# A second order of all operations of a recurrent-attention and max-out kernel

## Chip, cores and metric

The kernel runs on one core of a Trainium2 chip. The metric is the time of one execution on the device in microseconds (us), the median over runs. Lower is better.

## The reference

A recurrence with a state of 48x48 per batch and head goes through 768 steps (4 batches, 8 heads), and its output goes through a two-branch product with a maximum:

```python
for t in range(S):                                   # S = 768
    cur = einsum('bhd,bhe->bhde', u * k[t], v[t])
    y[t] = einsum('bhd,bhde->bhe', r[t], state + cur)
    state = w[t][..., None] * state + einsum('bhd,bhe->bhde', k[t], v[t])
x = y.transpose(0, 2, 1, 3).reshape(B * S, H * D)    # 3072 x 384
out = maximum(x @ w1, x @ w2) @ w_out                # d_ff = 1024
```

Inputs and outputs are float32.

## The kernel before

The sequence is cut into three chunks of 256 tokens. A unit of work is one chunk of one or two batches: units 0 to 3 are the first chunk of one batch each, unit 4 and 5 the second chunk of two batches each, 6 and 7 the third. The maximum is rewritten: `max(a, b) = relu(a - b) + b`, so that one product with `w1 - w2` (wd_sb) and a relu are followed by a product with w_out and one with `w2 @ w_out` (wc_sb), which the kernel works out itself once (wfold).

Nothing is ordered by a scheduler. A list of words, ORDER, names every operation and every load. A loop goes through it and issues each one to its engine, and each engine works through its own queue strictly in that order, waiting at the first operation whose inputs or buffer aren't there yet. The letter behind the @ chooses the engine where there is a choice (a is ACT, d is DVE, p is POOL):

```python
for o in ORDER:
    o, _, e = o.partition("@")
    name, *a = o.split(".")
    a = [int(x) if x.isdigit() else x for x in a] + ([e] if e else [])
    if name in ops:
        ops[name](*a)
    else:
        unit[name](U[a[0]], *a[1:])
```

The first number behind a unit's operation is the unit; the others are the batch in the unit, a half of the heads (unit 0 is done in halves) or a part. The operations, in the order in which a unit needs them, and the lines under which the profile has them:

- load.n.x: a load of w, k, r or v by SP's queue (L372). row and wl: one row of sums goes to memory and comes back on partitions (L472, L478). dt: a transpose by DMA (L582), in units 5 to 7. os: a store of the output (L743). All of these are in SP's one queue.
- hot.8: eight matmuls of 512 columns on zeros, whose result nobody reads (L234). They read the state buffer S_b that zero.s.0 clears (L263).
- zero.M, zero.k, zero.r, zero.v, zero.s, zero.m: buffers cleared once (L249 to L263). ident, tri, mask, identb, identq, trih: constants.
- wp: product of neighbouring w (L176, L180). ln: its logarithm on ACT (L387). ex: prefix sums by a matmul with a triangle on TensorE (L398; from unit 3 on two half-precision parts hi and lo, L395 and L396). mz: sums plus own logarithm on DVE (L440). e0 and ie: exponentials on ACT (L436, L460). wt, we: the decay over the chunk turned onto partitions by TensorE and its exponential by ACT, for units 0 and 1 (L466, L486); for the others we reads what wl brought (L488).
- rk, ru, dg, dd, di: the terms with u; dg is a row sum on DVE (L502), dd widens it, di sets it on the diagonal of the mask buffer M on DVE (L516). rw and kw: products with w. scale.n.0 and scale.n.1: r and k times their exponentials, into rp and kp. All of these products have the helper lines L176 and L180.
- vb: v to bf16. tr: transposes on TensorE (L565), and te: their copies on ACT. kv: keys times values (L596). st, sm, sb: the state carried on (L612, L615; S_f, S_b).
- sc: scores on TensorE into a Y buffer (L641). mk: the masked copy of them into M on DVE (L650). yi and ya: the output of the recurrence from the state and from M (L675, L688). xe: its copy xT (L168).
- wload, woload: loads of the three weight matrices. w2turn, w2take: w2 transposed. wdiff: w1 - w2 in three parts, wd_sb. wocast: w_out to bf16 in four parts, wo_sb. wfold, wctake: w2 @ w_out in three parts (L318) and their copies. u, uspread, utake: u on all partitions (L270).
- gt: xT times wd_sb (L706), which needs all three parts of wd_sb. rl: the relu (L717 on ACT, L719 on DVE). op: xT times wc_sb and gT times wo_sb (L725, L729). oe: the copy of its result (L168).

Two kinds of PSUM buffers serve TensorE: G has four (hot, ex, tr, w2turn, wfold, gt, op), Y has two (sc, kv, and the outputs of yi and ya). A buffer is taken again when the last operation that reads it is done.

Each ya multiplies 16 or 32 small tiles, each tr 8, each kv 32 or 64, each sc 16 (8 in unit 0), each gt 6 or 3, each op 11. A line of DVE, ACT or POOL at 168, 176 or 180 is that of the helper copy or mul, so the tile's name tells the operations apart.

Of the kernel before, what the change touches and what calls it, by code (L numbers as in the profile page):

```python
# [73 lines left out]
sc.2.0.1.0 mk.2.0.1.0 gt.0.1 mz.3.0 e0.3.0 kw.3.0@p gt.1.0 dg.3 sc.2.0.0.0 kv.2 st.2.0@a rl.0.1@a  # L74
wp.4.0@d ie.3.0 scale.3.0.0.0@d mk.2.0.0.0 wfold.2 sb.2.1@d wfold.0 dd.3@p ln.4.0 load.3.v st.2.1
wfold.1 sb.2.0@d vb.3.0@a wl.2 hi.4@a lo.4@d ya.2.0.0.0 load.4.r rl.1.0@a di.3.0@d vb.3.1@a row.3
ya.2.0.1.0 wctake.1@a we.2 load.4.k wctake.2@a rk.4.0@d wctake.0@a scale.3.1.0.0@p tr.3.0.0 ex.4.0
mz.4.0 tr.3.0.1 ex.4.1 mz.4.1 te.3.0.0@a kv.3 te.3.0.1@a st.3.0@a yi.2.0 xe.2.0@d ie.4.0 op.1.1
oe.1.1@a st.3.1 load.4.v e0.4.0 sb.3.0@a ru.4.0@d gt.2.0 load.5.w.0 rl.2.0@a sc.3.0.0.0 sc.3.0.1.0
vb.4.1@a gt.2.2 op.1.0 rk.4.1@p rw.4.0@d kw.4.0@d scale.4.0.0.0@d scale.4.1.1.0@d scale.4.1.0.0@p  # L80
e0.4.1 rl.2.2@a scale.4.0.1.0@d op.0.1 sb.3.1@a row.4 oe.1.0@a tr.4.1.0 te.4.1.0@a tr.4.1.1 vb.4.0@a
op.0.0 sm.2@p wl.3 mk.3.0.0.0 ya.3.0.0.0 mk.3.0.1.0 ya.3.0.1.0 yi.3.0 oe.0.1@d ru.4.1@p wp.5.0@p
we.3 sm.3@p te.4.1.1@a gt.2.1 xe.3.0@a dg.4 ln.5.0 oe.0.0@d tr.4.0.1 te.4.0.1@a gt.3.0 rl.3.0@a
rl.2.1@a hi.5@a dd.4@d load.5.k kv.4 di.4.0@d sc.4.1.1.0 load.5.r load.5.v rk.5.0@d gt.2.3 rl.2.3@a
gt.3.2 tr.4.0.0 di.4.1@d te.4.0.0@a mk.4.1.1.0 gt.3.3 st.4.0 st.4.1 os.1.0 rl.3.3@a gt.3.1 rl.3.1@a
ru.5.0@p sc.4.1.0.0 rk.5.1@p sc.4.0.0.0 load.6.r sb.4.0@a vb.5.1@a op.2.1 load.6.w.0 lo.5@d wl.4
ex.5.0 mk.4.0.0.0 os.0.0 sb.4.1@a mk.4.1.0.0 oe.2.1@a mz.5.0 e0.5.0 rw.5.0@p ex.5.1 sc.4.0.1.0
load.6.k ru.5.1@p mz.5.1 ya.4.0.0.0 scale.5.0.0.0@d op.2.0 rl.3.2@a op.3.0 mk.4.0.1.0 e0.5.1 os.1.1
scale.5.0.1.0@d dt.5.0.0 ya.4.0.1.0 dt.5.0.1 kw.5.0@d row.5 oe.3.0@d os.3.0 wp.6.0@p ie.5.0
# [19 lines left out]
rl.6.4@a op.6.0 sc.7.1.0.0 sb.7.0@a sc.7.1.1.0 op.6.2 di.7.1@d mk.7.1.1.0 op.6.3 yi.7.1 mk.7.1.0.0  # L109
yi.7.0 ya.7.0.0.0 oe.6.2@a ya.7.1.0.0 ya.7.1.1.0 ya.7.0.1.0 xe.7.0@d op.6.1 oe.6.3@a os.6.3 oe.6.0@d  # L110
os.5.3 os.6.2 oe.6.1@d xe.7.1@a gt.7.1 rl.7.1@d gt.7.0 gt.7.6 os.6.0 rl.7.0@a gt.7.2 gt.7.3 rl.7.2@a
rl.7.6@a rl.7.3@a os.6.1 gt.7.4 rl.7.4@a gt.7.7 rl.7.7@d gt.7.5 rl.7.5@d op.7.0 op.7.1 oe.7.0@d
# [685 lines left out]
```

## Time and profile before

| | |
|---|---|
| time, three runs | 146.47, 146.53, 146.93 us; median 146.53 |
| profiled execution | span 147.2 us from the first to the last instruction (no other time is given for it) |
| granted TensorE clock, mean | 0.987 |
| busy | PE 136.8 us, DVE 116.9, ACT 90.6, POOL 90.0 |
| queue of the loads and stores | 31.49 MB, its packets took 81.2% of the span of 16 DMA engines |

The page gives busy time and instructions by engine, then the span in 40 equal slices with the busy tenths of each, then the chain of work that ended last and the costliest groups by line. Rows of a timeline give start, duration, engine, line, operation, the tile written and read, and in square brackets the idle time ahead with what ended it. Rows of windows give the stretch and its length, then busy time of PE, PEld, DVE, ACT and POOL with the number of instructions, the granted clock, the share of the DMA engines and GB/s. Matmuls of one row overlap a little, so the start of the next row says when a row was done.

### The profile page before, as it was taken

What the parts mean: (1) busy time and instruction counts of PE and PEld (TensorE: products, weight loads), DVE (VectorE), ACT (ScalarE), POOL (GpSimd) and SP (SyncE); (2) the same over time, 40 slices, a digit from 0 to 9 for tenths busy, and PEclk for the clock granted to TensorE, in tenths of its full rate; (3) what the DMA queues carried; (4) which work ended last, traced back from release to release, by engine and by line L of the source; (5) the groups of instructions that cost most, each with busy time, mean ns of one, the idle gap of its engine ahead of it and who ended that gap; (6) DMA issues with size and microseconds to landing.
All of it is one profiled execution on the core that took longest, in us unless ns stands there. A gap on an engine that the chain in (4) does not pass through costs nothing.

```text
span 147.2 us, 5536 instructions
## 1 busy us (share of the span) xinstructions
PE 136.8 (93%) x2403; PEld 84.2 (57%) x2404; DVE 116.9 (79%) x162; ACT 90.6 (62%) x164; POOL 90.0 (61%) x106
## 2 busy tenths in 40 slices
PE   5999999779999999999999994999999999999990
...
DVE  2489999999999999999999967399967589361511
...
PEclk9999999999999999999999999599999999999999
...
GB/s 104 323 325 357 335 401 394 366 286 304 214 241 277 212 226 282 312 255 174 205 192 177 292 251 207 141 138 291 250 136 78 131 271 20 0 210 62 4 56 157
DMA packets 71186, 31.84 MB, mean 216 GB/s; under 512 B 66293, under 2 KB 70390, under 8 KB 71162
## 3 DMA queue, kind: packets, MB, share of 16 engines
q1 hardware_dynamic: 71162, 31.49, 81.2%
...
## 4 chain that ended last, share of the span: by engine, by line
PE 41%; DVE 35%; issue 6%; POOL 6%; DMA 4%; ACT 3%; SPq 2%; DVEq 0%; POOLq 0%; ACTq 0%
PE G L729 12%; DVE M L650 9%; PE G L706 8%; PE G L234 7%; PE G L725 5%; DVE rp L176 4%; DMA lv<-in_v_dram 4%; DVE rku L176 3%; DVE dg L502 3%; POOL kp L180 3%; DVE M L516 3%; PE Y L688 2%; SPq L582 2%; POOL rku L180 2%; PE Y L675 2%
## 5 line engine op out<-in xcount | busy, mean ns | idle before, releaser
L729 PE MATMUL G<-wo_sb,gT 128*128 128x384 bf16 x192 | 35.8, 331 | 0.0
L706 PE MATMUL G<-xT,wd_sb 128*128 128x256 bf16 (+1 forms) x192 | 34.4, 326 | 0.7 <-ACT xT L168 0.6
L650 DVE CAST_PREDICATED M<-mask,Y 128x1024 bf16<-128x1024 int32 (+1 forms) x26 | 28.6, 1131 | 2.8 <-PE Y L641 1.9
L717 ACT ACTIVATE gT<-G 128x512 bf16<-128x512 f32 x43 | 24.5, 601 | 9.8 <-PE G L706 9.6
L729 PEld LDWEIGHTS <-gT 128*128 128x128 bf16 x192 | 19.0, 99 | 12.6 <-issue 0.3
L706 PEld LDWEIGHTS <-wd_sb 128*128 128x128 bf16 x192 | 17.9, 98 | 12.6 <-DVE wd_sb L176 0.6
L180 POOL TENSOR_TENSOR kp<-lk,iE 128x384 bf16<-128x384 f32 x16 | 17.1, 1096 | 9.3 <-DVE lk L176 4.2
L725 PE MATMUL G<-wc_sb,xT 128*128 128x384 bf16 x72 | 15.7, 327 | 0.0
L180 POOL TENSOR_TENSOR rku<-rku,u_b 128x384 f32<-128x384 f32 x14 | 14.5, 1053 | 2.0 <-DVE rku L176 2.0
L234 PE MATMUL G<-S_b 128*128 128x512 bf16 x47 | 13.6, 442 | 1.8 <-DVE S_b L263 1.8
L168 ACT COPY RK<-G 128x1024 bf16<-128x1024 bf16 x12 | 12.1, 1019 | 4.7 <-PE G L565 4.7
L168 ACT COPY osb<-G 128x384 f32<-128x384 f32 x7 | 3.4, 479 | 15.9 <-PE G L729 12.6
L180 POOL TENSOR_TENSOR rku<-lr,lk 128x384 f32<-128x384 f32 x8 | 10.9, 1393 | 2.5 <-DMA lk<-in_k_dram 1.7
L641 PE MATMUL Y<-RK 48*64 48x128 bf16 x384 | 9.0, 220 | 2.6 <-DVE M L650 2.4
L502 DVE TENSOR_REDUCE dg<-rku 128x16 f32<-128x768 f32 x12 | 11.0, 945 | 0.1
L641 PEld LDWEIGHTS <-RK 48*64 48x64 bf16 x384 | 6.2, 106 | 7.8 <-issue 6.7
L168 ACT CAST xT<-Y 128x768 bf16<-128x768 f32 x7 | 7.0, 1025 | 5.3 <-PE Y L675 4.0
L168 ACT CAST S_b<-S_f 64x768 bf16<-64x768 f32 (+1 forms) x14 | 8.7, 624 | 2.3 <-DVE S_f L612 2.0
L176 DVE TENSOR_TENSOR rp<-lr,G 128x768 bf16<-128x768 f32 (+2 forms) x11 | 8.8, 799 | 1.4 <-ACT G L436 1.4
L234 PEld LDWEIGHTS <-S_b 128*128 128x128 bf16 x48 | 5.1, 112 | 8.3 <-issue 3.3
L516 DVE TENSOR_TENSOR M<-identq,gd 128x512 int32<-128x512 int32 x12 | 9.2, 778 | 0.4 <-POOL gd L168 0.3
L168 DVE CAST xT<-Y 128x768 bf16<-128x768 f32 x5 | 5.1, 1017 | 5.5 <-PE Y L688 3.2
(111 smaller groups left out, 240.2 us busy)
## 6 DMA issues: line engine op xcount, KB each, us to landing
...
```

The source lines that it names most:

```text
L168: (nc.scalar.copy if e == "a" else nc.vector.tensor_copy if e == "d" else nc.gpsimd.tensor_copy)(o, i)
L176: op(o, a, b)
L180: op(o[:, g], a[:, g], b[:, g])
L234: nc.tensor.matmul(t, zz[:, 0:P], zz[:, 0:512], start=True, stop=True)
L502: nc.vector.reduce_sum(s.dg[:, b].rearrange("p i h -> p h i"), s.rku[:, b], axis=AX.X)
L516: (nc.vector if en == "d" else nc.gpsimd).tensor_tensor(out=o, in0=m, in1=g.unsqueeze(3).to_broadcast([P, 2, H, Q // 2]), op=ALU.bitwise_and)
L641: nc.tensor.matmul(t[q * Q:(q + 1) * Q, e, p * P:(p + 1) * P].rearrange("s (i g) -> s i g", i=2), s.kT[d, b, j, y * n + p, q, :], s.rT[d, ...
L650: nc.vector.copy_predicated(t[:, :, 2 * n * y:2 * n * (y + 1)].rearrange("s i (p e) g -> s p e i g", e=2), mask[:, j].bitcast(I32).unsquee ...
L706: nc.tensor.matmul(t[:, m * n * P:(m + 1) * n * P].rearrange("c (b t) -> c b t", t=P), wd_sb[:, ko, fo * P:(fo + 1) * P], s.xT[:, 0:n, ko, :],
L717: nc.scalar.activation(o, i, AF.Relu)
L725: nc.tensor.matmul(t[:, 0:HD], s.xT[:, a, ko, :], wc_sb[:, ko, :], start=(ko == 0), stop=False)
L729: nc.tensor.matmul(t[:, 0:HD], s.gT[:, c:c + P], wo_sb[:, f, :], start=False, stop=(f == FO - 1))
```

## The change

The same 652 words stand in another order, and 89 of them carry another letter for their engine. Nothing else changes: the functions, the buffers, the arithmetic and the loads are the same. This is the diff, cut to the beginning (up to the first of the big products), unit 5 and 6, and the last tenth or fifth.

```diff
--- before.py
+++ after.py
@@ -51,66 +51,66 @@
 ORDER = """
-ident zero.s.1@p identq@a load.0.k load.0.r zero.m@p identb@p u zero.s.0@d zero.r@d rk.0.0@d
-load.0.w.1 load.0.w.0 wp.0.0@d hot.8.2 hot.8.3 load.2.w.0 zero.v.1@d wp.0.1@d mask ln.0.0 tri
-zero.k.1@p load.1.w.0 ln.0.1 ex.0.0 load.1.r kw.0.0@d mz.0.0 wp.2.0@d rw.0.0@d load.1.k zero.o@p
-load.0.v ie.0.0 uspread utake@a wp.1.0@d ex.0.1 ln.1.0 wload.1.0 mz.0.1 scale.0.1.0.0@p hot.8.0
-zero.M.1@p ie.0.1 load.3.w.0 ru.0.0@d dg.0 rw.0.1@p kw.0.1@p scale.0.1.0.1@p wt.0.0 ex.1.0 we.0.0
-e0.0.0 e0.0.1 wt.0.1 rk.1.0@d hot.8.5 vb.0.1@p load.2.r zero.v.2@d load.2.k load.1.v mz.1.0 ie.1.0
-rw.1.0@d wt.1.0 wload.1.2 ln.2.0 ex.2.0 vb.0.0@a we.0.1 scale.0.0.0.0@d zero.k.0@d kv.0
-scale.0.0.0.1@d tr.0.0.1 dd.0@p mz.2.0 woload.0 we.1.0 ru.1.0@p kw.1.0@p row.2 w2turn.0.0 e0.1.0
-scale.1.0.0.0@d st.0.0@a tr.0.0.0 te.0.0.1@a sc.0.0.1.1 sc.0.0.0.1 w2turn.0.1 dg.1 te.0.0.0@a
-w2take.0.0@a wload.0.2 load.2.v scale.1.1.0.0@d dd.1@p sb.0.0@a wp.3.0@p tr.1.0.1 e0.2.0 st.0.1
-te.1.0.1@a rk.2.0@d zero.M.2@p di.0.0@d ie.2.0 zero.M.0@p rw.2.0@d hot.8.1 wload.1.1 ru.2.0@d
-kw.2.0@p scale.2.1.0.0@p sc.0.0.1.0 sc.0.0.0.0 mk.0.0.1.0 vb.1.0@a hot.8.4 mk.0.0.0.0 mk.0.0.1.1
-mk.0.0.0.1 vb.1.1@a kv.1 scale.2.0.0.0@d tr.1.0.0 ln.3.0 te.1.0.0@a w2turn.2.1 wdiff.2@p sb.0.1@a
-st.1.0@a sb.1.0@a di.1.0@d st.1.1 tr.2.0.0 w2take.0.1@a tr.2.0.1 te.2.0.1@a zero.v.0@d sc.1.0.1.0
-w2turn.1.0 wload.0.0 wdiff.0@p w2take.1.0@a sc.1.0.0.0 mk.1.0.1.0 mk.1.0.0.0 sb.1.1@a w2take.2.1@d
-w2turn.2.0 w2turn.1.1 w2take.2.0@a hi.3@a ya.0.0.1.0 vb.2.1@a ya.1.0.0.0 sm.0@p sm.1@p wload.0.1
-wdiff.1@d ya.1.0.1.0 ya.0.0.0.1 load.3.r trih@a yi.1.0 yi.0.0 ya.0.0.0.0 woload.1 ya.0.0.1.1
-xe.1.0@a xe.0.0@d load.3.k te.2.0.0@a gt.1.3 rl.1.3@a dg.2 rk.3.0@d lo.3@d dd.2@a gt.0.2 rl.0.2@a
-wocast.1@p gt.1.1 w2take.1.1@d woload.3 gt.0.0 rw.3.0@p woload.2 rl.0.0@a gt.1.2 load.4.w.0 rl.1.2@a
-vb.2.0@p ru.3.0@p gt.0.3 rl.0.3@a ex.3.0 wocast.3@d wocast.2@a wocast.0@a rl.1.1@a di.2.0@d
...
-vb.5.0@a gt.4.7 rl.4.7@a we.4 sm.4@p gt.4.4 dt.5.1.0 gt.4.6 sc.5.0.1.0 mk.5.0.1.0 kv.5 oe.3.1@a
-rl.4.6@a rl.4.0@a rl.4.4@a st.5.0 gt.4.1 rl.4.1@a sc.5.0.0.0 mk.5.0.0.0 gt.4.3 rl.4.3@a dt.5.1.1
-rk.6.1@p st.5.1 ex.6.0 ru.6.1@p sb.5.1@a sb.5.0@a load.6.v os.0.1 vb.6.1@a mz.6.0 ex.6.1 op.4.3
-load.7.w.0 load.7.k mz.6.1 e0.6.1 ie.6.0 kw.6.0@d e0.6.0 scale.6.1.1.0@p di.5.1@d sc.5.1.0.0
-ya.5.0.1.0 rw.6.0@d ya.5.0.0.0 yi.5.0 xe.5.0@a vb.6.0@a scale.6.0.0.0@d op.4.2 wl.5 os.3.1
-scale.6.1.0.0@p sc.5.1.1.0 oe.4.2@a op.4.0 oe.4.3@a oe.4.0@a mk.5.1.0.0 wp.7.0@p ya.5.1.0.0
-mk.5.1.1.0 dt.6.0.0 ya.5.1.1.0 yi.5.1 kv.6 scale.6.0.1.0@d dt.6.0.1 xe.5.1@d st.6.0 dt.6.1.1 ln.7.0
...
-ya.6.0.1.0 os.5.2 os.4.0 ya.6.1.0.0 ya.6.0.0.0 oe.5.3@a os.4.3 kw.7.0@p scale.7.1.1.0@p
-scale.7.0.0.0@d ya.6.1.1.0 yi.6.0 xe.6.0@a scale.7.1.0.0@d dt.7.0.0 dt.7.1.0 yi.6.1 op.5.0 vb.7.0@p
-xe.6.1@a gt.6.5 oe.5.0@d os.5.0 e0.7.1 gt.6.3 rl.6.3@a rl.6.5@a scale.7.0.1.0@d dt.7.1.1 gt.6.2
-dt.7.0.1 os.4.2 kv.7 gt.6.6 gt.6.0 rl.6.6@a os.5.1 st.7.0 gt.6.1 rl.6.2@a ru.7.1@p dg.7 sb.7.1@a
-gt.6.7 rl.6.7@a rl.6.0@d sc.7.0.0.0 rl.6.1@a dd.7@p di.7.0@d sc.7.0.1.0 mk.7.0.1.0 mk.7.0.0.0 gt.6.4
...
+zero.M.0@d ident mask zero.o@p zero.k.0@d zero.s.0@d hot.8.2 load.0.r zero.m@p zero.r@p load.0.w.1
+load.0.w.0 identq@a wp.0.0@d wp.0.1@d ln.0.0 ln.0.1 zero.k.1@d load.0.k identb@p rw.0.0@d hot.8.0
+rk.0.0@d tri ex.0.0 mz.0.0 ex.0.1 mz.0.1 e0.0.1 load.2.w.0 wp.2.0@d zero.v.2@d kw.0.0@d ie.0.0
+scale.0.1.0.0@d hot.8.3 ie.0.1 u load.1.w.0 rw.0.1@d wt.0.1 kw.0.1@p wp.1.0@p scale.0.1.0.1@p
+load.0.v load.1.r uspread e0.0.0 scale.0.0.0.0@d utake@d zero.v.0@d scale.0.0.0.1@d hot.8.1 ln.2.0
+ex.2.0 ru.0.0@d wt.0.0 dg.0 dd.0@d load.1.k load.2.k we.0.0 ln.1.0 vb.0.1@d ex.1.0 rw.1.0@p kw.1.0@p
+mz.1.0 load.2.r tr.0.0.0 wload.1.2 load.1.v we.0.1 rk.1.0@d vb.0.0@a kv.0 tr.0.0.1 wload.1.1
+wload.1.0 te.0.0.0@a wt.1.0 we.1.0 di.0.0@d ru.1.0@d te.0.0.1@a ie.1.0 e0.1.0 sc.0.0.0.0 vb.1.0@a
+zero.s.1@p st.0.0@d sb.0.0@a sb.0.1@a mz.2.0 dg.1 e0.2.0 sc.0.0.1.0 woload.3 row.2 dd.1@a
+scale.1.0.0.0@d st.0.1 scale.1.1.0.0@p ie.2.0 hot.8.5 vb.1.1@a hot.8.4 w2turn.2.0 mk.0.0.1.0
+w2take.2.0@a kv.1 st.1.0@a sb.1.0@a tr.1.0.1 te.1.0.1@a w2turn.1.0 tr.1.0.0 load.3.w.0 wload.0.2
+mk.0.0.0.0 te.1.0.0@a w2turn.1.1 w2take.1.1@a zero.M.1@d st.1.1 wocast.3@a w2turn.2.1 w2take.1.0@a
+w2take.2.1@a rk.2.0@p kw.2.0@p sc.1.0.1.0 ru.2.0@p sc.1.0.0.0 di.1.0@d w2turn.0.1 sb.1.1@a
+w2take.0.1@a rw.2.0@d scale.2.1.0.0@d scale.2.0.0.0@d tr.2.0.1 w2turn.0.0 mk.1.0.1.0 mk.1.0.0.0
+woload.1 wocast.1@a ya.0.0.0.0 sc.0.0.0.1 sc.0.0.1.1 mk.0.0.1.1 tr.2.0.0 w2take.0.0@d te.2.0.0@a
+yi.0.0 mk.0.0.0.1 te.2.0.1@a dg.2 dd.2@a wp.3.0@p woload.2 wocast.2@p wload.0.0 woload.0 load.3.r
+wocast.0@a wdiff.2@p wload.0.1 wfold.2 wctake.2@a trih@a wfold.0 yi.1.0 ya.1.0.0.0 di.2.0@d
+ya.1.0.1.0 wdiff.0@d xe.1.0@a ln.3.0 wctake.0@a load.3.k wfold.1 rk.3.0@p kw.3.0@p sm.0@p ya.0.0.1.0
+wdiff.1@d ya.0.0.0.1 ya.0.0.1.1 hi.3@a gt.1.2 xe.0.0@d rl.1.2@a gt.1.1 load.3.v vb.3.0@a gt.0.1
+rl.1.1@a wctake.1@d load.2.v vb.2.1@a gt.1.0 rl.1.0@a vb.2.0@a load.4.w.0 lo.3@d load.4.r gt.1.3
+rl.1.3@a ex.3.0 ru.3.0@d gt.0.2 dg.3 dd.3@a sm.1@p sc.2.0.1.0 mz.3.0 e0.3.0 kv.2 st.2.0@a zero.M.2@d
+mk.2.0.1.0 rl.0.1@a load.4.k sb.2.1@a ie.3.0 op.1.1 sb.2.0@a wp.4.0@d di.3.0@d vb.3.1@a op.1.0
+rw.3.0@p ln.4.0 hi.4@a row.3 oe.1.1@d scale.3.0.0.0@d scale.3.1.0.0@p st.2.1 gt.0.0 rl.0.2@a
...
+sc.5.0.0.0 mk.5.0.1.0 mk.5.0.0.0 gt.4.7 e0.6.1 rl.4.7@a op.4.3 ex.6.0 di.5.1@d sc.5.1.0.0 os.2.1
+oe.4.3@a sc.5.1.1.0 op.4.2 mz.6.0 ie.6.0 os.0.0 e0.6.0 mk.5.1.0.0 ya.5.0.1.0 rw.6.0@p kw.6.0@p
+sb.5.1@a oe.4.2@a sb.5.0@a load.6.v wl.5 os.4.2 vb.6.1@a op.4.0 oe.4.0@a mk.5.1.1.0 load.7.k
+ya.5.1.1.0 ya.5.1.0.0 ya.5.0.0.0 scale.6.0.1.0@d scale.6.1.0.0@d scale.6.1.1.0@d dt.6.0.1 dt.6.1.1
+yi.5.0 xe.5.0@a wp.7.0@p yi.5.1 xe.5.1@d vb.6.0@a we.5 op.4.1 oe.4.1@a ln.7.0 gt.5.7 load.7.r
+scale.6.0.0.0@d dt.6.0.0 ru.6.1@d kv.6 st.6.0 gt.5.0 ru.6.0@p rl.5.7@a dt.6.1.0 rl.5.0@a dg.6 hi.7@a
+lo.7@d dd.6@d di.6.1@d gt.5.5 gt.5.4 rl.5.4@a os.4.1 rl.5.5@a rk.7.1@p di.6.0@d sb.6.0@d load.7.v
...
+ya.6.1.1.0 ya.6.1.0.0 ya.6.0.1.0 kw.7.0@d ru.7.0@p ya.6.0.0.0 scale.7.0.0.0@d dt.7.0.0 yi.6.0
+vb.7.1@a xe.6.0@a scale.7.1.0.0@p yi.6.1 op.5.0 xe.6.1@d gt.6.1 vb.7.0@a oe.5.0@a gt.6.3 gt.6.6
+ru.7.1@d scale.7.0.1.0@d dt.7.1.0 rl.6.6@a rl.6.3@a gt.6.4 rl.6.4@a scale.7.1.1.0@p kv.7 os.0.1
+gt.6.2 dt.7.0.1 dg.7 gt.6.0 rl.6.0@a sm.5@p st.7.0 sb.7.1@d gt.6.5 rl.6.5@a os.3.0 rl.6.2@a rl.6.1@a
+dd.7@p di.7.0@d sc.7.0.1.0 sc.7.0.0.0 mk.7.0.0.0 dt.7.1.1 gt.6.7 os.4.3 rl.6.7@a mk.7.0.1.0 sb.7.0@d
+op.6.3 oe.6.3@d sc.7.1.0.0 os.5.0 di.7.1@d mk.7.1.0.0 sc.7.1.1.0 op.6.2 op.6.0 yi.7.0 mk.7.1.1.0
+oe.6.0@a oe.6.2@d yi.7.1 ya.7.0.0.0 os.6.0 os.6.3 ya.7.0.1.0 os.4.0 ya.7.1.1.0 ya.7.1.0.0 xe.7.1@d
+op.6.1 xe.7.0@a gt.7.1 rl.7.1@a gt.7.3 rl.7.3@d gt.7.0 rl.7.0@a gt.7.4 gt.7.2 gt.7.5 rl.7.4@a
+oe.6.1@d os.6.1 gt.7.7 rl.7.2@d os.3.1 gt.7.6 os.6.2 os.5.1 rl.7.5@a rl.7.7@d rl.7.6@d op.7.0
+oe.7.0@d op.7.3 oe.7.3@d os.7.3 op.7.2 oe.7.2@a os.7.0 os.7.2 op.7.1 oe.7.1@a os.7.1
 """.split()
```

48 lines of the change are left out of this document (20 added, 28 removed).

## Prediction

> **What bounds the kernel now.** I read the page first, for busy shares and slices.
>
> ```profile
> span 147.2 us, 5536 instructions
> PE 136.8 (93%) x2403; PEld 84.2 (57%) x2404; DVE 116.9 (79%) x162; ACT 90.6 (62%) x164; POOL 90.0 (61%) x106
> PE   5999999779999999999999994999999999999990
> DVE  2489999999999999999999967399967589361511
> PEclk9999999999999999999999999599999999999999
> ```
>
> A slice is 3.68 us. The PE row is open at its two ends, a little around the ninth slice, and in the 25th, behind which the granted clock drops. Elsewhere TensorE has no room. VectorE is as full up to the 22nd slice and empties towards the end. A window of ten microseconds says the same in numbers (its length, then busy us of PE, PEld, DVE, ACT and POOL, the granted clock and the DMA share):
>
> ```profile
> 40.00:50.00 10.00, 10.00 (x208) 6.55 (x201) 9.96 (x16) 9.41 (x20) 6.84 (x6) 1.00 0.99 259
> ```
>
> Then TensorE's timeline, for when the full stretch begins, ends and is broken:
>
> ```profile
> 1.79 6.10 PE L234 MATMUL G<-S_b 128*128 128x512 bf16 x16 [1.79 <-DVE S_b L263]
> 14.66 0.95 PE L466 MATMUL G<-MZ 128*128 128x1 f32 x8
> 15.47 0.89 PE L398 MATMUL G<-lg,tri 128*128 128x384 f32 x2
> 33.11 4.28 PE L706 MATMUL G<-xT,wd_sb 128*128 128x256 bf16 x36 [0.60 <-ACT xT L168]
> 40.02 4.06 PE L318 MATMUL G<-wo_sb,wb 128*128 128x384 bf16 x24
> 87.29 1.46 PE L729 MATMUL G<-wo_sb,gT 128*128 128x384 bf16 x8
> 90.70 0.42 PE L641 MATMUL Y<-RK 48*64 48x128 bf16 x16 [1.94 <-DVE M L650]
> 142.37 1.46 PE L729 MATMUL G<-wo_sb,gT 128*128 128x384 bf16 x8
> ```
>
> So the kernel has three parts. Up to 33.11, when the first gt (the first of the two big products) starts, VectorE's queue sets the pace. From there to 143.83 TensorE runs through its queue with one real hole, at 88.75. The last 3.3 us are a copy and a store. TensorE's work is the same set of operations in both orders, so the new time is settled by when the first gt starts, how much of the queue is then done, and which holes lie behind it.
>
> **The change, part by part.** 28 operations go from POOL to DVE, 18 the other way, 17 from ACT to DVE, 20 back, 5 from POOL to ACT, 1 from ACT to POOL: 89. Priced start to start from the rows below, this gives DVE some 3 us more in all, POOL 12 less, ACT 2.5 more. DVE is not full behind 86 us and POOL nowhere, so the sums alone decide nothing; their places do.
>
> *Ahead of the first gt on TensorE.* The same operations as before, and in addition the three wfold, 24 matmuls and 4.06 us, which stood behind the gts. The new order breaks even if its first gt starts at 33.11 + 4.06 = 37.17.
>
> *The beginning.* DVE now clears M (512 words wide) and k (256) ahead of S_b, which the warm-up matmuls (hot) read.
>
> ```profile
> L263 DVE MEMSET S_b<- 128x768 uint32 x1 | 0.7, 698 | 1.0 <-PEq L782 1.0
> ```
>
> Together they are as wide as S_b: 0.7. The 16 hots stand ahead of the first prefix sums (ex.0.0) in both orders and take 6.10, so ex.0.0 moves from 1.79 + 6.10 = 7.89 to about 8.6, whatever the loads do. That w of unit 0 is now the second load instead of the fourth is hidden behind these hots; if it were not, it would be worth below 1 us.
>
> *Unit 1's sums.* On TensorE ex.1.0 now stands behind three more pieces: hot.8.3, hot.8.1 and ex.2.0; and on ACT its logarithm (ln.1.0) stands behind we.0.0, which reads wt.0.0, which TensorE does only after ex.2.0. Two rows of the chain and one of ACT's timeline complete the prices:
>
> ```profile
> 8.21 0.84 PE G L270 x2
> 9.57 1.73 PE G L234 x8
> 10.24 0.52 ACT L387 ACTIVATE lg<-lg 128x384 f32<-128x384 f32 x1 [0.68 <-DVE lg L176]
> ```
>
> From 8.6: the two half-wide sums 0.8, two blocks of hots 3.5, two halves of wt 0.8 (as the eight at 14.66, start to start), uspread 0.84, ex.2.0 at most 0.9: 15.4. Then ACT's few columns and ln.1.0, 0.6, and ex.1.0, 0.8: 16.8. VectorE's mz.1.0, half a us, can end at 17.2 or 17.3.
>
> *VectorE up to dg.2.* Prices are start to start:
>
> ```profile
> 8.99 0.35 DVE L176 TENSOR_TENSOR lw<-lr,lw 128x192 f32<-128x192 f32 x1
> 9.26 0.95 DVE L176 TENSOR_TENSOR lg<-lw 128x384 f32<-128x384 f32 x1
> 23.23 2.47 DVE L650 CAST_PREDICATED M<-mask,Y 128x512 bf16<-128x512 int32 x4
> 25.62 0.94 DVE L176 TENSOR_TENSOR rp<-lr,G 128x768 bf16<-128x768 f32 x1
> 28.45 2.28 DVE L650 CAST_PREDICATED M<-mask,Y 128x1024 bf16<-128x1024 int32 x2
> 30.65 0.68 DVE L168 CAST wb<-G 128x512 bf16<-128x512 f32 x1
> 33.53 0.93 DVE L502 TENSOR_REDUCE dg<-rku 128x16 f32<-128x768 f32 x1
> 45.26 0.68 DVE L516 TENSOR_TENSOR M<-identq,gd 128x512 int32<-128x512 int32 x1
> 45.86 0.94 DVE L176 TENSOR_TENSOR rku<-lr,lk 128x768 f32<-128x768 f32 x1
> 46.73 1.01 DVE L440 TENSOR_TENSOR MZ<-G,lg 128x384 f32<-128x384 f32 x2
> ```
>
> That is 0.27 for 192 wide, at most 0.5 for 384, 0.87 for 768 (a dg is within 0.06 of it), 0.60 for a di and for half a mask copy (2.39 / 4), 1.10 for a whole one (2.20 / 2). From the end of mz.1.0 to the end of dg.2 the new queue holds rk.1, ru.1, scale.1 (two halves), scale.2 twice, dg.1, dg.2: 8 x 0.87 = 7.0; di.0 and di.1 1.2; four half masks 2.4 and two whole 2.2; three st 0.8; mz.2.0, rw.2.0 0.95; zero.M.1 and w2take.0.0 (0.48, 0.60) 1.1. Sum 15.6. One wait is new: mk.0.0.1.1 reads a product that must wait for the Y buffer of mk.1.0.0.0, about 0.7 us for the copy to end and TensorE to fill it. 17.2 + 15.6 + 0.7 = 33.5 ends dg.2, against 34.46 before; slower pieces under POOL's traffic could put 0.8 on it, a shorter wait take 0.7 off.
>
> *The hole that this opens.* On ACT dd.2 (it reads dg.2) stands ahead of wocast.0, and every wfold begins with that quarter of w_out.
>
> ```profile
> L168 ACT CAST wo_sb<-wso 128x768 bf16<-128x768 f32 x2 | 1.6, 828 | 0.0
> 44.01 0.75 PE L688 MATMUL Y<-M,vp 64*32 64x128 bf16 x64
> ```
>
> wocast.0 therefore ends near 33.5 + 0.2 + 0.83 = 34.5. TensorE's queue ahead of wfold.2 ends with yi.0.0, bound by the same masks, near 31: some 3.5 us idle, where the row at 33.11 had 0.60. From 34.5: three wfold 4.06, and 112 ya with a yi between and behind them 1.4 (by the row, 0.75 for 64): the first gt starts at 40.0, 2.8 later than break-even. The bounds: with dg.2 0.7 sooner and smaller steps on ACT, +1.5; with POOL's drag, +3.6.
>
> *The clock.* What such a hole does further is seen at the other one, in chain and windows:
>
> ```profile
> 91.71 2.00 PE G L729 x8
> 96.73 1.30 PE G L729 x8
> 92.00:93.00 1.00, 1.00 (x6) 0.54 (x4) 1.00 (x2) 0.00 (x0) 1.00 (x2) 0.58 0.94 185
> 93.00:94.00 1.00, 1.00 (x35) 0.38 (x39) 0.25 (x1) 0.26 (x1) 1.00 (x2) 0.50 0.47 89
> 94.00:95.00 1.00, 1.00 (x72) 0.82 (x54) 0.00 (x0) 0.97 (x2) 0.01 (x1) 0.50 0.56 111
> 95.00:96.00 1.00, 1.00 (x52) 0.80 (x40) 0.47 (x1) 0.00 (x0) 0.00 (x0) 0.72 0.97 179
> ```
>
> After the idle time that ends at 90.70, 1.94 us, the granted clock falls to 0.50: eight matmuls take 2.00 instead of 1.30, and what the four windows lack of full speed adds to 0.42 + 0.50 + 0.50 + 0.28 = 1.7 us. The hole before wfold.2 is longer, so I take the same 1.7 there; the ends are 0 and twice it.
>
> The Trainium skill, "TensorE: Matmul & The Clock Gate", Part 1, says that the clock halves after an idle window of about 3.4 us, in windows that run free. Here 1.94 us of idle time sufficed, so by the trace a whole empty window isn't needed; by the page a hole of this length may or may not halve it, and the sum would be 1.7 lower where it doesn't.
>
> *The hole at 88.75.* Its chain: load.6.v lands late, vb.6.1 waits for it on ACT, behind it e0.6.0, for which VectorE's scale.6 waits, behind it the mask copy that frees TensorE's buffer.
>
> ```profile
> 79.96 6.14 DMA lv<-in_v_dram
> 86.17 0.83 ACT L168 CAST vp<-lv 128x768 bf16<-128x768 f32 x1 [0.90 <-DMA lv<-in_v_dram]
> 88.55 0.95 DVE L176 TENSOR_TENSOR rp<-lr,G 128x768 bf16<-128x768 f32 x1 [1.37 <-ACT G L436]
> ```
>
> In the new order both e0.6 stand ahead of vb.6.1 on ACT, and all four masks of unit 5 ahead of every scale.6 on VectorE. Both links are cut: -1.94 and -1.7, together -3.6; a new wait in their place could leave nothing of it. Late next are xe.5 and the transposes of unit 6, which op.4.1 and gt.5 cover by some 4 us.
>
> *The rest.* ACT has only 0.6 us free in the window 40:50, and dd.3 and e0.3.0 now stand among the first relus. From the masks of unit 4 on, new queues meet within half a microsecond; I take 0.5 for such waits, 0 to 3. SP's row.3 and row.4 hold back load.4.v and load.5.k by a few us, but their readers come 5 us later: nothing. The stores of units 0 and 3 move among the last; the stores of unit 7 keep the end of the queue, and the last copy goes from VectorE to ACT: nothing, the same 3.3 us.
>
> Sum: +2.8 + 1.7 - 3.6 + 0.5 = +1.4 on a span of 147.2. That span is 0.6 above the median of the runs, 146.53; the difference goes on the median: 147.9.
>
> **The rivals.** *The clock stays full* in the front hole. For it: no hole of this kind is in the front before, and the drop at 92 came with a delay. Against: a shorter hole sufficed. 147.9 - 1.7 = 146.2, on the edge of no change. *The front is as quick as before* (the other side): if dg.2 ends by 32 (products and masks of unit 0 ahead of where I put them), the hole shrinks below the 0.6 that was harmless; the first gt comes 1.5 sooner, without the clock's loss: 147.9 - 1.7 - 1.5 = 144.7. It decides from a dg.2 some 1.5 sooner than my walk. For it: xe.0.0 and wdiff.1, ahead of dg.2 in the old order, are behind it in the new. *VectorE becomes the bound late.* From unit 5's last mask to unit 7's, which in the run before are 92.4 and 126.4, the new queue has at these prices 4.9 us more VectorE work: it gains three scale.6, ru.6.1, rk.7.0, kw.7.0, ru.7.1 (7 x 0.87), xe.6.1 0.9, three sb 1.5, dd.6 and oe.6.3 0.7, and loses two ru and a scale 2.6, two relus 1.2, a copy 0.5.
>
> ```profile
> 92.40:126.40 34.00, 33.76 (x595) 19.36 (x593) 26.74 (x31) 19.29 (x33) 17.80 (x18) 0.95 0.72 156
> ```
>
> It was idle for 34.00 - 26.74 = 7.3 there, so about 2 us are to spare, and xe.6.1, sb.7 and oe.6.3 on it now wait for TensorE with masks behind them. From 2 us of such waits on it costs one for one; 2 more give 149.9.
>
> **How the numbers follow.** Forecast 0.42 (146.9 to 149.0 by itself), full clock 0.20 (145.6 to 146.7), quick front 0.20 (144.0 to 145.6), late bound 0.18 (149 to 151.5). A measurement here tells about 0.3% from no change: 146.1 to 147.0. Faster: the quick front and 0.4 of the full clock, 0.28; the same: the rest of that and a little of the forecast, 0.15; slower 0.57. Half of each outer case left out gives 144.7 to 150.0.
>
> **What would show it.** Right: ex.0.0 near 8.6, dg.2 ending near 33.4, a TensorE idle of 3 us or more before L318 released by ACT, a granted clock near 0.5 behind it, the first L706 at 40 to 42, no hole near 88. Wrong: L706 before 38.5; a clock of 1.00 throughout; a new wait of TensorE above 1 us behind 45; or VectorE without idle time in 95 to 125.

## Result and profile after

| | before | after |
|---|---|---|
| time, median (lowest to highest), us | 146.50 (146.33 to 146.93) | 158.55 (157.50 to 160.27) |
| ratio | | 1.079 (1.074 to 1.084) |

A run more than 1.5% above the fastest of its kernel counts as slow and is left out of the ratio and of all medians below; of the four runs of the changed kernel that is the profiled one, and the other three have a median of 157.97.

The changed kernel is thus 11.5 us slower. Slower was forecast, a time near 158 was not: the range ended at 150.0.

In every run of this study the time is about 1.7 us (1.66 to 1.89) above the span. The profiled execution of the changed kernel (span 158.6, time 160.3) is 2.3 above its median; the profile of before, with its span of 147.2, belongs to an execution of about 148.9, some 2.4 above *its* median (seven later runs of the old kernel have spans of 144.3 to 146.4). The prediction had taken span for time.

The page of the changed kernel, span, busy line, and the slices of PE, DVE and the granted clock:

```profile
span 158.6 us, 5533 instructions
PE 142.2 (90%) x2403; PEld 86.6 (55%) x2404; DVE 129.1 (81%) x169; ACT 93.4 (59%) x171; POOL 81.5 (51%) x89
PE   3999699493999999995699999999999999999991
DVE  3469999989649999999997899999998978933510
PEclk9999999958699999999659999999999999999999
```

A slice is 3.97 us here. Two places are open in the PE row, at 28 to 40 us and at 71 to 79, and the clock drops in or behind both. The busy line already points at the cause: VectorE was forecast to get some 3 us more work (116.9 to 120) and has 129.1.

TensorE's timeline, the rows that answer to those of before and the new idle times:

```profile
2.60 6.26 PE L234 MATMUL G<-S_b 128*128 128x512 bf16 x16 [2.60 <-DVE S_b L263]
31.57 0.40 PE L565 MATMUL G<-identb,rp 128*128 128x128 bf16 x4 [1.78 <-DVE rp L176]
38.30 4.44 PE L318 MATMUL G<-wo_sb,wb 128*128 128x384 bf16 x16 [2.60 <-ACT wo_sb L168]
45.58 3.45 PE L706 MATMUL G<-xT,wd_sb 128*128 128x256 bf16 x30
75.29 0.42 PE L641 MATMUL Y<-RK 48*64 48x128 bf16 x16 [1.90 <-DVE T L615]
78.12 0.48 PE L396 MATMUL G<-wst 128*128 128x384 f16 x1 [1.16 <-DVE wst L413]
```

The first gt starts at 45.58, 8.4 us behind break-even (37.17). Behind it the old hole near 88 is gone, and a costlier one stands at 73 to 79. The stretch behind the first gt has grown by (158.6 - 45.6) - (147.2 - 37.2) = 3.0, and 8.4 + 3.0 is the whole difference of the two spans, 11.4. VectorE's timeline of the same profile shows the operations that were priced in the prediction:

```profile
9.82 1.25 DVE L176 TENSOR_TENSOR lg<-lw 128x384 f32<-128x384 f32 x1
13.39 1.15 DVE L176 TENSOR_TENSOR lw<-lr,lw 128x192 f32<-128x192 f32 x1
26.54 1.16 DVE L516 TENSOR_TENSOR M<-identq,gd 128x512 int32<-128x512 int32 x1
28.90 1.75 DVE L176 TENSOR_TENSOR kp<-lk,iE 128x768 bf16<-128x768 f32 x1
30.57 0.94 DVE L176 TENSOR_TENSOR rp<-lr,G 128x768 bf16<-128x768 f32 x1
36.32 0.95 DVE L502 TENSOR_REDUCE dg<-rku 128x16 f32<-128x768 f32 x1
```

192 columns take 1.15 instead of 0.35, 768 take 1.75. But the product with an operand in PSUM (G) and the row sum take what they did before. GpSimd's timeline shows what ran beside the first of them:

```profile
9.65 1.00 POOL L176 TENSOR_TENSOR lg<-lw 128x384 f32<-128x384 f32 x1 [1.14 <-DMA lw<-in_w_dram]
12.15 1.10 POOL L176 TENSOR_TENSOR lw<-lr,lw 128x384 f32<-128x384 f32 x1
13.28 1.05 POOL L176 TENSOR_TENSOR lw<-lk,lw 128x384 f32<-128x384 f32 x1
```

### The profile page after: what moved, and what is told of

It is laid out like the page before. It is cut to its first block, busy times and chain, and to the rows that moved or that the text cites. A ratio compares the mean times of both kernels' runs of the same rounds, so it can differ in the third digit from the quotient of the medians.

```text
span 158.6 us, 5533 instructions
## 1 busy us (share of the span) xinstructions
PE 142.2 (90%) x2403; PEld 86.6 (55%) x2404; DVE 129.1 (81%) x169; ACT 93.4 (59%) x171; POOL 81.5 (51%) x89
## 4 chain that ended last, share of the span: by engine, by line
PE 49%; DVE 11%; issue 1%; ACT 0%
PE G L729 16%; PE G L706 15%; PE G L725 7%; PE Y L688 4%; PE Y L641 3%; DVE rku L176 2%; PE Y L675 2%; DVE M L650 1%; PE Y L596 1%; DVE rp L176 1%; DVE dg L502 1%; DVE wst L413 1%; PE G L396 1%; DVE M L516 1%; DVE wst L202 1%
## 5 line engine op out<-in xcount | busy, mean ns | idle before, releaser
L706 PE MATMUL G<-xT,wd_sb 128*128 128x256 bf16 (+1 forms) x192 | 35.5, 335 | 0.4 <-DVE osb L168 0.4
L180 POOL TENSOR_TENSOR kp<-lk,iE 128x384 bf16<-128x384 f32 x12 | 14.4, 1230 | 20.9 <-ACT iE L460 7.7
L180 POOL TENSOR_TENSOR rku<-lr,lk 128x384 f32<-128x384 f32 x12 | 14.7, 1246 | 9.2 <-DMA lr<-in_r_dram 6.3
L168 ACT COPY osb<-G 128x384 f32<-128x384 f32 x11 | 5.3, 478 | 13.0 <-PE G L729 13.0
L168 ACT CAST xT<-Y 128x768 bf16<-128x768 f32 x8 | 8.2, 1027 | 6.9 <-PE Y L688 3.6
L516 DVE TENSOR_TENSOR M<-identq,gd 128x512 int32<-128x512 int32 x12 | 11.0, 922 | 0.4 <-ACT gd L168 0.3
L176 DVE TENSOR_TENSOR rku<-rku,u_b 128x768 f32<-128x768 f32 x9 | 10.6, 1181 | 0.0
L168 ACT CAST vp<-lv 128x768 bf16<-128x768 f32 (+1 forms) x15 | 10.2, 679 | 0.0
L688 PE MATMUL Y<-M,vp 64*32 64x128 bf16 x768 | 9.4, 226 | 0.0
L688 PEld LDWEIGHTS <-vp 64*32 64x32 bf16 x768 | 7.4, 92 | 3.5 <-issue 3.1
```

The source lines that it names most:

```text
L168: (nc.scalar.copy if e == "a" else nc.vector.tensor_copy if e == "d" else nc.gpsimd.tensor_copy)(o, i)
L176: op(o, a, b)
L180: op(o[:, g], a[:, g], b[:, g])
L688: nc.tensor.matmul(lhsT=s.vp[g, b, 2 * p + e, j, m * 32:(m + 1) * 32], rhs=s.M[b, j][g, :, 2 * p + e, :], **into(s, b, q, p * 96 + (e + m) ...
L706: nc.tensor.matmul(t[:, m * n * P:(m + 1) * n * P].rearrange("c (b t) -> c b t", t=P), wd_sb[:, ko, fo * P:(fo + 1) * P], s.xT[:, 0:n, ko, :],
```

## Experiments

### Order or letters: e1 and e2

e1 is the new order with every letter as before; e2 is the old order with the new letters.

> The new order of all words with the old letters, so that the 89 operations are back on their old engines. If the order itself makes the time (theory: its first big product starts 8.4 us later than the break-even of 37.2, and the back loses 3.1 us more than before), it stays above 155 us. If the moved letters make it (rival: they put DVE's two-input work beside POOL's), it falls below 150 us. Between these both count.

> The old order with the new letters. If the order makes the time, 147 to 149 us. If the letters do, 153 us or more, with stretched DVE rows in the trace.

Measured: e1 174.87, ratio 1.191 (1.184 to 1.197); e2 174.16 from the one run that counts (the other three 176.97 to 179.23), no ratio. Read by the bounds set for them, e1 (above 155) says that the order makes the time and e2 (153 or more) that the letters do. Both can't be the whole cause, and both times lie so far above the changed kernel itself that neither reading holds. The longest idle times of TensorE in e1:

```profile
33.58 0.61 PE L565 MATMUL G<-identb,rp 128*128 128x128 bf16 x4 [5.57 <-DVE rp L176]
107.81 0.64 PE L641 MATMUL Y<-RK 48*64 48x128 bf16 x16 [5.04 <-DVE T L615]
```

An order and its letters fit only each other; the loss of the pair is not a sum of one and the other.

### Front or back: e3 and e4

e3 has the old words and letters up to the first gt, then the remaining new ones; e4 the reverse.

> The old order with its old letters up to the first gt, then all remaining words in the new order with the new letters. Theory (the beginning costs 8.4 of 11.6 us): 148.5 to 150.5 us. Rival (the beginning's lateness would be made up for behind it, and the new order's later queue is what costs): 154 us or more.

> The new order with its new letters up to the first gt, then all remaining words in the old order with the old letters. Theory (the beginning costs 8.4 us): 153.5 to 156 us, with the first gt near 45.5 us. Rival (the later queue costs): below 150 us.

Measured: e3 156.75, ratio 1.068 (1.061 to 1.075); e4 159.36, ratio 1.084 (1.078 to 1.091). e3 has the time of its rival, though not by its reason alone, and e4 is slower than both of its ranges. e3's timeline of TensorE:

```profile
32.22 0.43 PE L688 MATMUL Y<-M,vp 64*32 64x128 bf16 x32
36.92 5.74 PE L318 MATMUL G<-wo_sb,wb 128*128 128x384 bf16 x24 [4.28 <-ACT wo_sb L168]
42.50 3.44 PE L706 MATMUL G<-xT,wd_sb 128*128 128x256 bf16 x30
```

The old front stands, and still the first gt is 5.3 late against 37.17: three wfold ahead of the gts, on a w_out that ACT casts too late, are expensive by themselves. Behind the first gt e3 takes 155.0 - 42.5 = 112.5 us, against 113.0 in the changed kernel and 110.0 before. e4 got no old back either: behind the new front the old words opened a hole.

```profile
56.76 1.07 PE L688 MATMUL Y<-M,vp 64*32 64x128 bf16 x64 [3.51 <-DVE M L650]
```

So neither cut separates front and back cleanly.

### Single places of the front: g1, g2, g3

All three are the changed kernel with a few words moved.

```diff
 g1:  -vb.1.0@a zero.s.1@p st.0.0@d      +ex.1.0 zero.s.1@p rw.1.0@p kw.1.0@p
 g2:  +hot.8.6 ahead of tr.2.0.1         +hot.12.7 behind yi.0.0
 g3:  +woload.2 wload.0.0 woload.0 ahead of ya.0.0.0.0, wocast.0@a ahead of te.2.0.0@a
      -woload.2 wload.0.0 woload.0 wocast.0@a behind dd.2@a
```

> The new order with one word moved: zero.s.1, a clearing of POOL's (1.38 us), ahead of POOL's rw.1.0 and kw.1.0 instead of behind them. Theory (a DVE operation with two SBUF inputs is stretched while POOL works on two inputs; in the new order rw.0.1 takes 1.15 us beside them instead of 0.35): rw.0.1 shrinks by 0.8, mz.1.0 on DVE starts 0.8 to 1.5 us sooner than 18.5, and the kernel gains 0.5 to 1.5 us. Rival (DVE there waits for TensorE's sums, behind the warm-up blocks): mz.1.0 stays at 18.5, the time does not change.

Measured: 158.28, ratio 1.084 (1.076 to 1.091). With GpSimd clearing a buffer beside it (1.37 us) instead of multiplying, the product of 13.39 is back at its price:

```profile
11.85 0.35 DVE L176 TENSOR_TENSOR lw<-lr,lw 128x192 f32<-128x192 f32 x1
```

mz.1.0 starts at 16.45 instead of 18.54, but 0.85 of that is the warm-up: the 16 hots took 5.41 here and 6.26 in the profile above. The whole doesn't get faster by an amount that can be told.

> The new order with idle time of TensorE filled: eight more warm-up matmuls ahead of tr.2.0.1 (hole of 1.8 us) and twelve behind yi.0.0 (hole of 2.6 us). Theory (holes halve the granted clock for some 3.4 us each, 1.7 us lost each time): the clock stays at 1.00 from 30 to 44, the sixteen matmuls of the first two wfold take 2.7 instead of 4.4 us, first gt at 43.5 to 44, 1.5 to 2.5 us gained. Rival (the clock is not what costs, since the masks and differences on DVE bound the first gt anyway): first gt stays within 0.5 of 45.6 and the time within 0.7 us.

Measured: 158.92, ratio 1.083 (1.077 to 1.089). The clock is full:

```profile
38.42 2.76 PE L318 MATMUL G<-wo_sb,wb 128*128 128x384 bf16 x16 [0.30 <-ACT wo_sb L168]
44.02 3.45 PE L706 MATMUL G<-xT,wd_sb 128*128 128x256 bf16 x30
```

Sixteen wfold matmuls take 2.76 instead of 4.44, and from the first of them to the first gt it is 5.60 instead of 7.28: 1.7 less, the size of the prediction's term. The time is the same all the same. The fillers themselves held up a score that a mask waits for: VectorE waits 2.92 us for it instead of 0.74, and the first gt, at 44.02, is no sooner than g1's at 43.95, behind a warm-up of nearly the same length. Behind it TensorE waits for VectorE at 73.67, 1.55 us (1.90 in the changed kernel). So g2 shows the size of the term, and not what a full clock without fillers would be worth.

> The new order with wocast.0 on ACT ahead of the two copies te.2 and dd.2 (SP's queue unchanged). Theory (the wfolds wait for ACT, which waits for DVE's dg.2): the hole of 2.6 us ahead of wfold.2 is gone or below 0.7, wfold.2 starts near 35.8, and the first gt comes near 42.2, when DVE has finished wdiff.1: 2.5 to 4 us gained. Rival (wocast.0 waits for its load as long): wfold.2 above 37.5 and no change.

Measured: 155.96, ratio 1.065 (1.057 to 1.072): 2.0 faster than the changed kernel, a little less than the 2.5 expected at least. TensorE's idle time ahead of wfold.2 is gone, and the first gt starts at 42.79 (42.2 expected); the late hole is not gone:

```profile
35.34 4.61 PE L318 MATMUL G<-wo_sb,wb 128*128 128x384 bf16 x16
72.48 0.42 PE L641 MATMUL Y<-RK 48*64 48x128 bf16 x16 [1.88 <-DVE T L615]
```

### The old hole: g4

The old kernel with vb.6.1 moved behind e0.6.0 on ACT.

```diff
-load.6.v os.0.1 vb.6.1@a mz.6.0
+load.6.v os.0.1 mz.6.0 ... e0.6.0 vb.6.1@a
```

> The old kernel with one word moved: vb.6.1 on ACT behind e0.6.0 instead of ahead of mz.6.0. Theory (the late load of v holds ACT, behind it e0.6 and scale.6, behind them the mask copy and TensorE: a hole of 1.94 us and 1.7 of halved clock): hole and clock drop at 88 to 96 are gone, 143 to 144.5 us. Rival (the next late thing takes its place, the masks behind scale.6.0.0.0 or the transposes): 145.5 us or more.

Measured: 146.13 against 146.51, ratio 0.997 (0.995 to 0.999). The hole shrinks as the chain in the prediction said, and the clock stays full:

```profile
89.51 0.42 PE L641 MATMUL Y<-RK 48*64 48x128 bf16 x16 [0.66 <-DVE M L650]
```

But only 0.4 us come of it, not the 2 to 3.5 of the theory, since in most executions of the old kernel the clock is full anyway (1.00 or 0.996 in the runs beside it, 0.987 in the profile of before). The idle time is shorter in them too, as far as one trace tells: q0 below, with vb.6.1 in its old place, has 0.97 us there, at full clock. The 3.6 that the prediction credited belonged to one execution. Of the kernels with all of the work in them, this small variant is the only one that beats both.

### The disputed cost by itself: m1

Twelve stages of six VectorE operations, alone and beside GpSimd.

```python
DVE.tensor_mul(rr, ab, bb)                        # two: 128x768, both from SBUF
DVE.tensor_mul(rr[:, 0:512], ab[:, 0:512], Q)     # psum: Q in PSUM
DVE.tensor_copy(rr, ab)                           # one
DVE.tensor_reduce(rr[:, 0:16], ab..., op=add)     # sum
POOL.tensor_mul(pr[:, 0:384], pa[:, 0:384], pb[:, 0:384])   # x10; or copies x10, memsets x16
```

> The disputed cost by itself; the kernel computes nothing of the reference and stores zeros. Twelve stages, each with six VectorE operations on 128x768 (128x512 where one operand is in PSUM) alone or beside ten or more GpSimd operations on 128x384. Theory A (two engines that both read two operands from SBUF hold each other up): the product of two SBUF operands takes 0.87 us start to start alone and 1.3 to 1.8 beside GpSimd's products, 0.87 beside GpSimd's copies and memsets; with one operand in PSUM, a copy or a row sum on VectorE are not drawn out. Rival B (the long products in the changed kernel come from something else there, the loads or their own operands): 0.87 in every stage, within 0.1.

VectorE's timeline, in order: two alone, beside products, beside copies, beside memsets; psum alone, beside products; one alone, beside products; sum alone, beside products.

```profile
5.13 5.92 DVE L65 TENSOR_TENSOR rr<-ab,bb 128x768 f32<-128x768 f32 x6 [1.67 <-DMA bb<-in_k_dram]
11.72 10.11 DVE L65 TENSOR_TENSOR rr<-ab,bb 128x768 f32<-128x768 f32 x6
26.27 7.14 DVE L65 TENSOR_TENSOR rr<-ab,bb 128x768 f32<-128x768 f32 x6
35.88 5.92 DVE L65 TENSOR_TENSOR rr<-ab,bb 128x768 f32<-128x768 f32 x6
43.76 4.28 DVE L67 TENSOR_TENSOR rr<-ab,Q 128x512 f32<-128x512 f32 x6
48.70 4.29 DVE L67 TENSOR_TENSOR rr<-ab,Q 128x512 f32<-128x512 f32 x6
59.70 3.53 DVE L69 COPY rr<-ab 128x768 f32<-128x768 f32 x6
63.89 7.71 DVE L69 COPY rr<-ab 128x768 f32<-128x768 f32 x6
76.04 5.89 DVE L71 TENSOR_REDUCE rr<-ab 128x16 f32<-128x768 f32 x6
82.59 5.89 DVE L71 TENSOR_REDUCE rr<-ab 128x16 f32<-128x768 f32 x6
```

Theory A holds for the products: 0.99 each alone, 1.69 beside GpSimd's products, 0.99 beside its memsets; PSUM operands and row sums go free. It was wrong on two points: GpSimd's copies also cost VectorE something (1.19), and VectorE's own copy is drawn out most of all, 0.59 to 1.29. GpSimd's rows, beside two and then alone:

```profile
11.68 14.20 POOL L76 TENSOR_TENSOR pr<-pa,pb 128x384 f32<-128x384 f32 x10
93.55 10.62 POOL L76 TENSOR_TENSOR pr<-pa,pb 128x384 f32<-128x384 f32 x10
104.52 5.62 POOL L78 COPY pr<-pa 128x384 f32<-128x384 f32 x10
```

A product of each, 0.99 + 1.06 = 2.05 one after the other, takes 1.69 as a pair; a VectorE copy with a GpSimd product 1.29 instead of 0.59 + 1.06 = 1.65; a VectorE product with a GpSimd copy 1.19 instead of 0.99 + 0.56 = 1.55. GpSimd's ten, less those that it did alone behind VectorE's last, come to some six beside VectorE's six in each of these stages (estimated from the rows), so the two engines take turns, and 0.36 us of a pair overlaps. The Trainium skill, "SBUF — State Buffer", "Who interferes with whom", says that VectorE instructions with two SBUF inputs (against GpSimd instructions that read SBUF) and its copies in a two-port mode share one port pair with GpSimd, and that row sums and single-input work outside those modes do not. The stages agree, the copy included. The Trainium skill also says there that the loser is blocked for the whole instruction; by that a pair would take an estimated 2.05, the sum of the lone durations, and 1.69 was measured.

### What contention is worth here: q1, q0, q3

In all three every product or difference on GpSimd copies its first operand and leaves the second factor out:

```diff
-        n = 1
+        n, op = 1, op if e == "d" else lambda o, a, b: nc.gpsimd.tensor_copy(o, a)
```

q1 is the changed kernel with it, q0 the old one, q3 the changed one with g3's moves as well.

> The changed kernel, but every product and difference on GpSimd copies its first operand only: the second factor is left out, order, letters and all else stay. Theory A (VectorE is late because GpSimd's products draw out its own): VectorE's products get back their lone durations, dg.2 ends about 3 us sooner than 37.2, the idle times of TensorE near 75 and 78 go, and the whole takes 5 to 7 us less, 151 to 153.5; the idle time before wfold.2 stays, since wocast.0 still stands behind dd.2. Rival B (the new order itself makes VectorE late): less than 1.5 us less, above 157, with the hole near 75 as before.

> The control: the old kernel, with the second factors of GpSimd's products and differences left out as in the kernel before this. Theory A (the new order has more of the contention on its path): the old kernel gains less, 1 to 3 us, since VectorE's row is drawn out by some 3.6 us in its front and TensorE alone decides behind it: 143.5 to 145.5. Rival (the omission makes every kernel faster by the same, and has nothing to do with the change): 5 us or more, below 141.5.

> The changed kernel with wocast.0 ahead of te.2 and dd.2 on ACT, and GpSimd's second factors left out. If contention and wocast.0's place are two causes that add, 151.9 - 2.6 to 3.0 = 148.9 to 149.3, with no idle time of TensorE ahead of wfold.2. Rival (TensorE waits for VectorE's masks as soon as the wait for wocast.0 is gone): 150.5 to 152.

Measured: q1 151.86, ratio to the old kernel 1.034 (1.026 to 1.042); q0 145.56, 0.993 (0.989 to 0.996); q3 148.18, 1.008 (1.004 to 1.012). q1 and q0 came out as theory A had it, q3 as the two causes that add, 0.7 us better. The busy line of q0:

```profile
PE 134.4 (93%) x2403; PEld 83.3 (58%) x2404; DVE 114.4 (80%) x162; ACT 90.6 (63%) x164; POOL 54.0 (38%) x106
```

Where its first gt starts:

```profile
32.58 4.28 PE L706 MATMUL G<-xT,wd_sb 128*128 128x256 bf16 x36 [0.61 <-ACT xT L168]
```

The busy line of q1:

```profile
PE 136.8 (92%) x2403; PEld 84.5 (57%) x2404; DVE 117.9 (79%) x169; ACT 93.1 (62%) x171; POOL 42.2 (28%) x89
```

q1's timelines, of VectorE and of TensorE:

```profile
32.77 0.95 DVE L502 TENSOR_REDUCE dg<-rku 128x16 f32<-128x768 f32 x1
```

```profile
34.76 4.18 PE L318 MATMUL G<-wo_sb,wb 128*128 128x384 bf16 x16 [3.00 <-ACT wo_sb L168]
72.17 0.42 PE L641 MATMUL Y<-RK 48*64 48x128 bf16 x16 [0.60 <-DVE M L650]
```

And TensorE's timeline of q3:

```profile
32.95 2.76 PE L318 MATMUL G<-wo_sb,wb 128*128 128x384 bf16 x16 [0.78 <-ACT wo_sb L168]
38.55 3.45 PE L706 MATMUL G<-xT,wd_sb 128*128 128x256 bf16 x30
```

Without the second factors VectorE's busy time falls by 129.1 - 117.9 = 11.2 in the new order and by 116.9 - 114.4 = 2.5 in the old one; between the two it differs by 3.5, the "some 3" of the prediction. The omission also makes GpSimd itself faster, but no idle time of TensorE, VectorE or ACT over 0.3 us in the changed kernel was ended by GpSimd.

The 11.5 us split so: with the second factors left out in both kernels the difference is 151.86 - 145.56 = 6.3, so these factors make 5.2, give or take 1.5 by the intervals of the ratios. This is not all of the contention, since the copies in their place still cost VectorE's products 0.20 us each in m1. wocast.0's place makes 151.86 - 148.18 = 3.7 of the rest (2.0 in g3, where VectorE is late anyway); 2.6 remain, of which 1.9 are in the first gt (q3's 38.55 against q0's 32.58 + 4.06) and the others are not explained.

### The late hole: h1 and h3

```diff
 h1:  kv.4 rl.2.3@a +st.4.0 +st.4.1 dg.4 dd.4@d -di.4.0@d ... -st.4.0 ... -st.4.1 ... ex.5.1 +di.4.0@d di.4.1@d
 h3:  the same, and ru.4.1@d -> @p, sm.3@d -> @p, hi.5@d -> @a
```

> The changed kernel with three words moved on VectorE's queue near 70 us: both st.4 (they free the buffer for which TensorE waits 1.90 us) ahead of dg.4, and di.4.0 behind lo.5 (for which TensorE waits 1.16). No work is added or taken. Theory P (their place in the queue is the cost): both waits go, and with them the half clock behind them, 3.3 + 3.4 us: 151.5 to 153. Rival A (VectorE as a whole is late there, 16 us without idle time, so that something else is late next): TensorE waits instead for the first mask of unit 4 ahead of its ya (L688, released by DVE M), which ends no sooner, and the time stays within 1.5 us of 158.5.

> As the kernel with the three moved words, and in addition three operations get back their old letter: ru.4.1 and sm.3 to GpSimd, hi.5 to ACT, 1.75 + 1.16 + 1.25 = 4.2 us off VectorE ahead of the masks of unit 4. Rival A of the former kernel (the amount of work on VectorE): now the holes from 73 to 79 and the half clock behind them go, 3 to 6.5 us less, 152 to 155.5. Theory P: the same time as the former kernel, 151.5 to 153, within 0.5 of it.

Measured: h1 157.54, ratio 1.070 (1.062 to 1.079); h3 159.95, ratio 1.089 (1.080 to 1.099). h1 went as rival A said: the wait for T is gone, and a longer one for a mask stands behind it (at a score, which needs the buffer that the mask reads, and not at a ya).

```profile
73.98 0.32 PE L396 MATMUL G<-wst 128*128 128x384 f16 x1 [1.33 <-DVE wst L413]
78.11 0.64 PE L641 MATMUL Y<-RK 48*64 48x128 bf16 x16 [2.50 <-DVE M L650]
```

h3 missed. VectorE lost 4.2 us of work, and spent it waiting for hi.5, which ACT, in its own order, made only at 75:

```profile
75.40 1.53 DVE L413 SCALAR_TENSOR_TENSOR wst<-lg,wst 128x768 f16<-128x768 f32 x1 [3.05 <-ACT wst L200]
```

So less work on VectorE was not tried cleanly here; that the lateness is contention rests on q1, where the wait for T is gone, that for lo.5 is 0.18 instead of 1.16, and the longest left there is 0.60 for a mask.

### The lesson on the old order: g5

g4, and di.1.0 moved from behind scale.2.0 to directly behind di.0.0, out of GpSimd's differences.

> The old kernel with vb.6.1 behind e0.6.0 on ACT, and in addition di.1.0 moved on VectorE from behind scale.2.0 to directly behind di.0.0. There GpSimd clears a buffer instead of multiplying, so that di.1.0 should take 0.68 instead of 1.50, and the masks of unit 1, yi.1 and the first gt come up to 0.8 sooner: 145.3 to 145.9 against 146.1. Rival (another operation of VectorE falls beside GpSimd's products in its place, or the loads hold the first gt): 146.1 within 0.3.

Measured: 146.50, ratio 0.998 (0.995 to 1.001), no gain over g4. The rival comes nearer, 0.1 outside its range: two di now take 1.28 instead of 0.68 + 1.50, but the masks of unit 0 behind them come later, so does the product that ACT copies next, and VectorE waits for that copy, 0.86 us.

```profile
21.44 1.28 DVE L516 TENSOR_TENSOR M<-identq,gd 128x512 int32<-128x512 int32 x2
28.18 0.36 DVE L615 TENSOR_TENSOR T<-Y,S_f 128x192 f32<-128x192 f32 x1 [0.86 <-ACT S_f L168]
```

## Why the prediction was wrong, point by point

- *Break-even and beginning*: right. ex.0.0 started at 8.70 (8.6 forecast).
- *VectorE up to dg.2*: **this step failed.** It priced each product at its undisturbed duration and gave GpSimd's traffic 0.8 for the whole stretch. dg.2 ended at 37.3 instead of 33.5, 3.8 late; mz.1.0 was 1.9 of that late already, because VectorE itself was behind, not for ex.1.0. With GpSimd's second factors left out dg.2 ends at 33.7: the walk through the queue was right, the prices were not. A part of this is the warm-up, which differs between executions. dg.2's end less the length of the sixteen hots is 27.4 in the forecast, 31.0 in the changed kernel, 30.0 to 30.3 in e4, h1 and h3, which have the same words up to there, and 28.0 in q1 and q3: 2 to 3 us are GpSimd's second factors. The quoted rows had the warning in them: 0.95 for 384 columns at 9.26, where 768 elsewhere take 0.94.
- *The hole before wfold.2*: mechanism right (g3), idle 2.60 where 3.5 was forecast. Another of 1.78 at 31.57 was not foreseen.
- *The clock*: it dropped as forecast, and 1.7 is its size from wfold.2 to the first gt (g2). g2 had it full there and still took 158.92, so *the clock stays full* was no way to 146.2. What it is worth by itself stays open; in q3 the same stretch takes 5.60 instead of q1's 7.01, part of a first gt 3.2 sooner and a time 3.7 shorter.
- *The hole at 88.75*: gone, as forecast; the credit of 3.6 failed. It was read from one execution 2.4 above the median and then subtracted from the median. g4 puts it near 0.4. With that alone the prediction's own terms give 146.5 + 2.8 + 1.7 - 0.4 + 0.5 = 151.1.
- *The rest*, 0.5 (0 to 3): **failed, and by the same step**, products of VectorE priced without what runs beside them. The hole at 73 to 79 is 1.90 + 0.20 + 1.16 = 3.3 us idle, and the 6.64 busy us in the window of 76 to 84 below lack 6.64 x (1 - 0.57) = 2.9 of full speed: 6.2 against the 3.6 of the old hole. The difference, 2.6, is most of the 3.0 by which the stretch behind the first gt has grown. VectorE has no idle time to speak of from 58 to 79, in either kernel; in the new order contention makes it late there (q1). Between the two profiled spans the forecast was 2.8 + 1.7 = 4.5 up to the first gt and -3.1 behind it, and 8.4 and 3.0 were measured: the larger part of the miss lies behind.
- *VectorE becomes the bound late*: right in kind, wrong in place. At the times that the prediction named VectorE is nearly full, and TensorE doesn't wait (second row; both are windows of the changed kernel). The stage itself lies some 11 us later here, from 103.4 to 138.6, and TensorE is busy for 35.08 of its 35.20 us:

```profile
76.00:84.00 8.00, 6.64 (x127) 3.86 (x125) 7.86 (x9) 3.15 (x5) 6.25 (x5) 0.57 0.63 157
92.40:126.40 34.00, 33.88 (x715) 19.65 (x714) 33.12 (x41) 23.94 (x43) 23.19 (x22) 1.00 0.94 211
```

- *The front is as quick as before*: wrong; it needed a dg.2 that ends at 32.
